# Two heads per step, softmax division after the product, and transfers in the order of the source: sparse attention feeding an expert layer

## The chip, the cores and the metric

The kernel runs on one core of one Trainium2 chip. The metric is the device time of one execution in microseconds (us), as the median of several runs. The engines are TensorE (PE in the profile; PEld is its loading of stationary operands), VectorE (DVE), ScalarE (ACT), GpSimd (POOL) and SyncE (SP), which here only issues transfers. SP's queue is written SPq.

## The reference

There are 8 batches of 8 heads, 576 queries and keys per head, 64 columns per head. Attention keeps only the scores that lie within tau (0.02) of the row's largest, and its output goes into an expert layer of 512 x 2048 x 512.

```python
scores = scale * np.matmul(q, k.transpose(0, 1, 3, 2))
thresh = np.max(scores, axis=-1, keepdims=True) - tau
scores = np.where(scores >= thresh, scores, -1000000000.0)
scores = scores - np.max(scores, axis=-1, keepdims=True)
attn = np.exp(scores)
attn = attn / (np.sum(attn, axis=-1, keepdims=True) + 1e-09)
attn_out = np.matmul(attn, v)
...
x = attn_out.transpose(0, 2, 1, 3).reshape(B * S, H * D)
h = x @ w_in
g = h * (1.0 / (1.0 + np.exp(-h)))
return g @ w_out
```

Because a score decides by a threshold whether a key counts at all, the kernel computes with values split into a high and a low part, which together carry more digits than one 16-bit or one fp32r value.

## The kernel before

**Visits and tiles.** Attention is worked off in visits. A visit is one pair of heads of one batch, and it is cut into tiles of 128 queries: four full ones for each head and a ninth that holds the last 64 queries of both heads. Batches 1 to 7 have four such visits each ("all"). Batch 0 has its visits in two halves, "low" (the first 256 queries) and "high" (the rest), so that the experts can start early; between them lie 12 free slots in which weights are decoded and split.

**Scores.** For one head, the high and the low part of q are stacked in the 128 partitions (64 rows each, `qstack`, made by `split_q`, lines 294 to 313), and k's high and low part (`split_k`, 315 to 321) each lie twice. So a tile needs two stationary loads of 128 rows per half of the keys: four matmuls of 128x128x288, or eight in the shared tile (`scores`, 385 to 409). For the stacking each of q and k is loaded twice from HBM (`load_qk`, 280 to 287).

**Softmax.** A tile takes these steps: DVE finds the row maximum (416) and the threshold (419); ACT takes the exponent (426); DVE masks and sums in one instruction (435) and inverts the sum (439, 443); ACT multiplies the row with it (448); POOL (ACT in the first 36 tiles) rounds to 16 bits (459) and subtracts for the low part (462, 465). SP then issues a transposing transfer (475) into `wT`. The scores tile `s` has two buffers of two PSUM banks; `w` has four buffers, `hl` three.

**Product with v and experts.** `av` (480 to 495) multiplies the transposed weights with v's two parts, both heads side by side in the array's columns, 128x64 each, in two ranges of 288 queries. `av_post` splits the result into x's two parts. The experts come as units: `h_unit` (12 matmuls, then tanh and two more steps), and quarters of `o_unit` (12 matmuls each). The units of a batch run while attention of the next batch goes on.

**Order.** The program is written as a loop over slots, one tile each (695 to 738). In each slot, softmax steps, planned loads and splits (`todo`), a number of expert units (`credit`) and products with v (`avs`) are emitted. The order on every engine is then set by a scheduler that simulates the program, with higher priority for scores and softmax. That includes the order of transfers in SP's queue. An engine, SP too, carries out its instructions strictly in that order, and one that waits holds those behind it.

The first visits ("low") work with plain fp32 scores and transposes on TensorE (`load_direct`, `scale_direct`, `soft3_direct`, `av_direct`).

Of the kernel before, what the change touches and what calls it, by code (L numbers as in the profile page):

```python
# [19 lines left out]
P = 128  # L20
# [6 lines left out]
WID = 320  # L27
EXPMASK = 0x7F800000
GB = 17  # buffers of g: a group of 16 and one ahead
WSPARE = 2  # raw weights lie this far ahead of the split ones, which take their place  # L30
LOAD = 5  # tiles that the loads of q and k run ahead
AV_LAG = 3  # tiles from a visit's last to its product with v
EARLY = 36  # tiles in which ACT still rounds the weights of attention for GpSimd
GAP, GAP1 = 12, 1  # free slots before batch 0's second visits and before batch 1
V_SLOT = 26  # batch 0's values are split from here on
# [6 lines left out]
# a visit of two heads: its tiles of 128 queries (4: the last 64 of both heads) for the  # L42
# first and the second head, and the query ranges that it completes
VISITS = {
    "low": ([0, 1], [0, 1], [(0, 256)]),
    "high": ([2, 3, 4], [2, 3], [(256, 320)]),
    "all": ([0, 1, 2, 3, 4], [0, 1, 2, 3], [(0, 288), (288, 288)]),
}
# [3 lines left out]
def attention_moe(  # L52
# [14 lines left out]
    xp = [ctx.enter_context(tc.tile_pool(name="x0", bufs=1))]  # L67
    stage_ctx = ExitStack()
    stage = stage_ctx.enter_context(tc.tile_pool(name="stage", bufs=2))
    ps_s = ctx.enter_context(tc.tile_pool(name="ps_s", bufs=2, space=PSUM))  # L70
# [3 lines left out]
    # three banks in turn; the last one is for the sums of the weights while they come in  # L74
# [20 lines left out]
    # stacks of (hi; lo) rows of q, with 64 zero columns for the shared tile  # L95
    qstack = []
    zeros = const.tile([P, 64], F32, name="zeros")
    nc.vector.memset(zeros, 0.0)
    for i in range(2):
        t = const.tile([P, S + 64], F32R, name=f"qstack{i}")  # L100
        zc = S if i % 2 == 0 else 0
        nc.vector.tensor_copy(t[:, zc : zc + 64], zeros)
        qstack.append(t)
# [32 lines left out]
    # ---------------------------------------------------------------- weights  # L136
# [47 lines left out]
        # sums of the magnitudes over the rows of four chunks, four columns at a time: they  # L184
        # bound h (w_in), w_out
# [33 lines left out]
    # ---------------------------------------------------------------- values  # L219
# [5 lines left out]
    def load_v(b, p):  # L225
        t = sb.tile([P, 2, 5, D], F32, tag="vraw", name=f"vraw_{b}_{p}", bufs=5)
        nc.sync.dma_start(out=t, in_=vL[b, :, 2 * p : 2 * p + 2])
        vraw[b, p] = t
# [37 lines left out]
    def split_v(b, p):  # L266
        t = vraw[b, p]
        s = vsc[b][:, 0:1]
        o = sb.tile([P, 2, 2, 5, D], F16, tag="v16", name=f"v16_{b}_{p}", bufs=4)
        nc.scalar.activation(o[:, 0], t, AF.Copy, scale=s)  # L270
        nc.vector.scalar_tensor_tensor(
            out=o[:, 1], in0=t, scalar=s, in1=o[:, 0], op0=ALU.mult, op1=ALU.subtract
        )
        v16[b, p] = o

    # ---------------------------------------------------------------- q and k
    qkraw = {}
    khl = {}

    def load_qk(v, h):  # L280
        b, hh = divmod(h, H)
        qr = sb.tile([P, S], F32, tag="qraw", name=f"qraw_{v}_{h}", bufs=2)
        kr = sb.tile([P, S], F32, tag="kraw", name=f"kraw_{v}_{h}", bufs=2)
        for r in range(2):
            nc.sync.dma_start(out=kr[r * D : (r + 1) * D, :], in_=kT[b, hh])
            nc.sync.dma_start(out=qr[r * D : (r + 1) * D, :], in_=qT[b, hh])
        qkraw[h] = qr, kr

    def qcol(h, i):
        """Column of query tile i in the stack (even: 0..3, last, zeros; odd: zeros, last,  # L290
        2, 3, 0, 1)."""
        return i * P if h % 2 == 0 else (0, 384, 512, 128, 256)[(i + 1) % 5]

    def split_q(h, tiles):
        qr = qkraw[h][0]
        odd = h % 2
        c0, c1 = 0, S
        if len(tiles) < 4:
            c0, c1 = (0, 320) if odd else (256, S)
# [45 lines left out]
    def soft3_direct(t):  # L345
# [4 lines left out]
        for k in range(4):  # L350
            nc.tensor.transpose(main[:, k, :], w[:, k * P : (k + 1) * P], ident)
# [429 lines left out]
```

## Time and profile before

| | |
|---|---|
| median of 3 runs | 1354.81 us (1354.6 to 1356.63) |
| span of the profiled execution | 1360.4 us |
| TensorE busy | 1183.7 us, 87% of the span |
| VectorE busy | 1002.8 us, 74% |
| ScalarE busy | 817.5 us, 60% |
| GpSimd busy | 789.9 us, 58% |
| DMA engines, mean busy share of the one large queue | 55.5% |
| mean granted TensorE clock | 0.950 of full speed |

The profile is of one execution. Busy times are unions of instruction times; matmuls are pipelined, and a busy PE is not one at its peak. A group row gives the source line, the engine, the operation, what is written and read, the shapes and the count; after the bar the busy time in us, the mean duration of one in ns, and the idle time of the engine just before them with what ended it.

### The profile page before, as it was taken

The numbers are of one execution on the slowest core, as the hardware profiler recorded it, in microseconds if no ns is written. First come the engines' busy times: TensorE is split into PE (matmuls) and PEld (weight loads), VectorE is DVE, ScalarE is ACT, GpSimd is POOL, SyncE is SP. The second block draws the span as 40 slices with busy tenths as digits, with TensorE's granted clock in tenths as the row PEclk, the third lists the DMA queues.
The fourth block names the chain that finished last, engine by engine and source line by source line (L and its number), as shares of the span: only waits on it lengthen the run. The fifth ranks groups of instructions, "written<-read, shape, count | busy, mean of one in ns | idle before, by whom it ended". The sixth has DMA issues, their size and how long they took to land.

```text
span 1360.4 us, 26858 instructions
## 1 busy us (share of the span) xinstructions
PE 1183.7 (87%) x9392; PEld 899.9 (66%) x9392; DVE 1002.8 (74%) x2619; ACT 817.5 (60%) x1493; POOL 789.9 (58%) x964
## 2 busy tenths in 40 slices
PE   3774787898599979898899969899799999999998
PEld 2453555666477757676677757677577777777777
DVE  4987997897598967968497856869478787872421
ACT  3776775675476756656375745757367666662432
POOL 2647984787478656754476646556467666661000
PEclk9887888999799999999899979999799999999999
DMA  6454955778467656664475556565466565543000
GB/s 226 140 185 125 197 129 94 146 139 170 88 133 155 122 106 129 131 128 86 99 132 124 118 96 136 101 127 121 82 122 116 115 129 115 106 88 53 6 19 18
DMA packets 363479, 158.15 MB, mean 116 GB/s; under 512 B 329552, under 2 KB 338256, under 8 KB 363344
## 3 DMA queue, kind: packets, MB, share of 16 engines
q1 hardware_dynamic: 363344, 156.43, 55.5%
q8 instruction: 74, 1.21, 0.4%
q14 instruction: 61, 0.50, 0.1%
HBM read 66.72 MB, written 9.44 MB: 56 GB/s over the span
## 4 chain that ended last, share of the span: by engine, by line
DVE 35%; PE 34%; issue 13%; ACT 6%; POOL 6%; DMA 5%; SPq 2%; POOLq 0%; ACTq 0%; DVEq 0%
PE o L562 15%; PE h L524 8%; DVE w L435 8%; DVE sm L416 6%; DVE gbuf L547 6%; PE s L406 5%; PE a L490 5%; DVE qstack L310 3%; DVE th L533 3%; DMA vraw<-in_vL 2%; DMA wT<-hl 2%; ACT w L426 2%; POOL hl L459 2%; POOL hl L462 2%; ACT w L448 2%
## 5 line engine op out<-in xcount | busy, mean ns | idle before, releaser
L524 PE MATMUL h<-x,wst 128*128 128x288 f16 (+2 forms) x3072 | 422.3, 290 | 22.6 <-DVE th L533 19.1
L562 PE MATMUL o<-gbuf,wst 128*128 128x288 f16 (+2 forms) x3072 | 419.4, 293 | 22.4 <-DVE gbuf L547 16.1
L562 PEld LDWEIGHTS <-wst 128*128 128x128 f16 x3072 | 296.4, 100 | 117.1 <-issue 27.1
L459 POOL TENSOR_SCALAR hl<-w 128x576 f16<-128x576 f32 x264 | 187.3, 710 | 317.9 <-ACT w L448 69.1
L524 PEld LDWEIGHTS <-wst 128*128 128x128 f16 x3072 | 290.7, 99 | 119.2 <-issue 37.5
L462 POOL TENSOR_TENSOR hl<-w,hl 128x512 f16<-128x512 f32 x272 | 332.0, 1220 | 28.0 <-issue 13.9
L426 ACT ACTIVATE w<-s,sm 128x576 f32<-128x576 f32 x288 | 211.0, 736 | 204.5 <-POOL hl L465 135.4
L435 DVE SCALAR_TENSOR_TENSOR w<-s,sm,w 128x576 f32<-128x576 f32 x288 | 232.6, 810 | 110.4 <-ACT w L426 108.7
L448 ACT ACTIVATE w<-w,sm 128x576 f32<-128x576 f32 x288 | 218.2, 770 | 86.5 <-DVE sm L443 81.6
L416 DVE TENSOR_REDUCE sm<-s 128x1 f32<-128x576 f32 x288 | 215.1, 748 | 44.4 <-PE s L406 42.3
L406 PE MATMUL s<-khi,qstack 128*128 128x288 f32 x608 | 160.4, 346 | 70.0 <-DVE w L435 36.9
L547 DVE SCALAR_TENSOR_TENSOR gbuf<-th,gbuf 128x288 f16<-128x288 f32 (+2 forms) x256 | 167.3, 656 | 20.9 <-ACT gbuf L541 20.2
L406 PEld LDWEIGHTS s<-khi,qstack 128*128 128x128 f32 x608 | 98.5, 198 | 98.8 <-issue 71.4
L490 PE MATMUL a<-wT,v 128*64 128x288 f16 (+1 forms) x1680 | 142.4, 294 | 16.1 <-DMA wT<-hl 15.0
L532 ACT ACTIVATE th<-h,msc 128x288 f32<-128x288 f32 (+2 forms) x256 | 126.3, 495 | 49.5 <-DVE gbuf L547 30.0
L541 ACT ACTIVATE gbuf<-th 128x288 f16<-128x288 f32 (+2 forms) x252 | 109.9, 438 | 44.5 <-DVE th L533 43.9
L406 PE MATMUL s<-klo,qstack 128*128 128x288 f32 x608 | 134.2, 304 | 0.0
L533 DVE SCALAR_TENSOR_TENSOR th<-th,h 128x288 f32<-128x288 f32 (+2 forms) x256 | 113.2, 444 | 27.6 <-ACT th L532 25.4
L490 PEld LDWEIGHTS <-v 128*64 128x64 f16 x1680 | 91.3, 110 | 56.7 <-issue 41.9
L465 POOL TENSOR_TENSOR hl<-w,hl 128x64 f16<-128x64 f32 x272 | 115.3, 424 | 0.0
L406 PEld LDWEIGHTS s<-klo,qstack 128*128 128x128 f32 x608 | 102.2, 197 | 0.0
L320 POOL TENSOR_TENSOR klo<-kraw,khi 128x576 fp32r<-128x576 f32 x64 | 95.6, 1493 | 1.4 <-ACT khi L318 1.3
(82 smaller groups left out, 868.8 us busy)
## 6 DMA issues: line engine op xcount, KB each, us to landing
qraw<-in_qT SPq DMA_DIRECT2D x128, 144.0 KB, 3.0
kraw<-in_kT SPq DMA_DIRECT2D x128, 144.0 KB, 3.0
vraw<-in_vL SPq DMA_DIRECT2D x32, 320.0 KB, 3.5
wraw<-in_w_out SPq DMA_DIRECT2D x16, 512.0 KB, 4.0
out_t<-ot SPq DMA_DIRECT2D x56, 144.0 KB, 2.0
wT<-hl SPq DMA_TRANSPOSE x304, 3.3
gbuf<-in_w_in SPq DMA_DIRECT2D x8, 512.0 KB, 5.1
wraw<-in_w_in SPq DMA_DIRECT2D x8, 512.0 KB, 4.9
```

The source lines that it names most:

```text
L406: nc.tensor.matmul(s_ps[:, j, :HALF], lhs, kk[:, j * HALF : (j + 1) * HALF], start=(n == 0), stop=(n == len(seq) - 1),)
L416: nc.vector.tensor_reduce(out=negm, in_=s_ps[:, :, :HALF], op=ALU.max, axis=AX.XY, negate=True)
L426: nc.scalar.activation(wtile[t].rearrange("p (j c) -> p j c", j=2), sps[t][:, :, :HALF], AF.Exp, bias=small[t][:, 0:1],)
L435: nc.vector.scalar_tensor_tensor(out=w3, in0=s_ps[:, :, :HALF], scalar=sm[:, 1:2], in1=w3, op0=ALU.is_ge, op1=ALU.mult, accum_out=sm[:, 2:3],)
L448: nc.scalar.activation(w, w, AF.Copy, scale=r)
L459: nc.gpsimd.tensor_scalar(out=fl[:, 0:S], in0=w, scalar1=1.0, scalar2=1.0, op0=ALU.mult, op1=ALU.mult)
L462: nc.gpsimd.tensor_tensor(out=fl[:, 640:1152], in0=w[:, 0:512], in1=fl[:, 0:512], op=ALU.subtract)
L490: nc.tensor.matmul(a_ps[odd * D : (odd + 1) * D, :n], vt[:, lo_v, odd, kv, :], wT[v, b * H + 2 * p + odd][:, kw, c0 - base : c0 - base + n ...
L524: nc.tensor.matmul(ph[:, :n], wi(c, f, lo_w), x16[b, lo_x][:, c, c0 : c0 + n], start=(k == 0), stop=(k == 11),)
L533: nc.vector.scalar_tensor_tensor(out=th[:, :n], in0=th[:, :n], scalar=1.0, in1=ph[:, :n], op0=ALU.add, op1=ALU.mult,)
L547: nc.vector.scalar_tensor_tensor(out=g[:, 1, :n], in0=th[:, :n], scalar=2.0**-14, in1=g[:, 0, :n], op0=ALU.mult, op1=ALU.subtract,)
L562: nc.tensor.matmul(ps[:, :n], wo(f, d, lo_w), g[:, lo_g, :n], start=(f == 0 and k == 0), stop=(f == NF - 1 and k == 2),)
```

## The change

1. **Both heads of a pair in one step.** A step is one tile of 128 queries of both heads (or the shared tile of the last 64 queries, as before). The pair's q and k lie one head in partitions 0 to 63, the other in 64 to 127, so they are loaded once and split once per visit. The four products of high and low parts become four matmuls of 64 rows per head and half of the keys, and the heads alternate. The maximum, the rounding and the subtraction cover both heads (1152 columns) in one instruction; exponent and masked sum stay one per head. A step takes two slots, the shared one takes one slot.
2. **Buffers.** `s` has one buffer of four banks; `w` two and `hl` two buffers of both heads; raw q and k have one each. In the loop, the scores of the next step are now emitted behind the masked sums of the step.
3. **Division per visit.** Weights are no longer divided row by row. The sums of a range of queries are collected, inverted at once (`invert_sums`), written to DRAM in pieces of 4 bytes, read back three slots later, spread over 64 partitions per head (`load_rows`), and multiplied with the result of the product with v on DVE; ACT rounds it and POOL subtracts. The "low" visits still divide by row.
4. **Engines.** The threshold moves from DVE to POOL, rounding of the weights from POOL to ACT, x's low part from DVE to POOL.
5. **Values.** The 1152 transposed rows of a head (576 high, 576 low) now lie without a gap, so that v's high part is needed a second time, moved by 64 rows; two transfers inside SBUF make it. v is loaded once for its maximum and once more for its splitting.
6. **Ranges** are 256 and 320 queries for all visits; the product follows five slots behind.
7. **Transfers.** SP's queue is in the order of the source (`manual_schedule`); the other engines are still ordered by the scheduler.

The core of the diff:

```diff
+    ctx.enter_context(tc.manual_schedule(engines={mybir.EngineType.SP}))
...
-    ps_s = ctx.enter_context(tc.tile_pool(name="ps_s", bufs=2, space=PSUM))
+    ps_s = ctx.enter_context(tc.tile_pool(name="ps_s", bufs=1, space=PSUM))
...
     def scores(t):
-        v, parts = tiles[t]
-        s_ps = ps_s.tile([P, 2, 512], F32, tag="s", name=f"s_{t}")
+        v, i = steps[t]
+        s_ps = ps_s.tile([P, 2, 2, 512], F32, tag="s", name=f"s_{t}")
...
+            qh, ql, kh, kl = qk16[v]
+            seq = [(qh, kh), (qh, kl), (ql, kh), (ql, kl)]
+        w = P if i == 4 else D
+        for n, (qq, kk) in enumerate(seq):
             for j in range(2):
...
+                for h in range(heads(t)):
+                    r = slice(h * w, (h + 1) * w)
+                    nc.tensor.matmul(
+                        s_ps[:, h, j, :HALF], qq[r, i * P : (i + 1) * P],
+                        kk[r, j * HALF : (j + 1) * HALF],
+                        start=(n == 0), stop=(n == len(seq) - 1),
+                    )
...
+            out=sm[:, 0:nh], in_=s_ps[:, :nh, :, :HALF], op=ALU.max, axis=AX.XY, negate=True
+        )
+        nc.gpsimd.tensor_scalar(
+            out=sm[:, 2 : 2 + nh], in0=sm[:, 0:nh], scalar1=-1.0, scalar2=ntau,
+            op0=ALU.mult, op1=ALU.add,
+        )
...
+        nc.scalar.activation(hl[:, :nh, 0:S], w[:, :nh], AF.Copy)
         nc.gpsimd.tensor_tensor(
...
+            out=hl[:, :nh, S : 2 * S], in0=w[:, :nh], in1=hl[:, :nh, 0:S], op=ALU.subtract
+        )
```

The new functions for the sums:

```python
def invert_sums(v, a, b):
    if v not in rdram:
        r = sb.tile([P, 9], F32, tag="rsum", name=f"rsum_{v}", bufs=2)
        rdram[v] = r, dram.tile([2, S], F32, tag="rs", name=f"rs_{v}", bufs=4)
    r, d = rdram[v]
    nc.vector.tensor_scalar(
        out=r[:, a:b], in0=sums[v][:, a:b], scalar1=1e-9, scalar2=None, op0=ALU.add
    )
    nc.vector.reciprocal(out=r[:, a:b], in_=r[:, a:b])
    for h in range(2):
        if a < 8:
            nc.sync.dma_start(
                out=d[h, 64 * a : 64 * min(b, 8)].rearrange("(i p) -> p i", p=P),
                in_=r[:, a + h : min(b, 8) : 2],
            )
        if b == 9:
            nc.sync.dma_start(
                out=d[h, S - D :].rearrange("(p o) -> p o", o=1),
                in_=r[h * D : (h + 1) * D, 8:9],
            )

def load_rows(v, g):
    c0, n = RANGES[g]
    _, d = rdram[v]
    R = sb.tile([P, WID], F32, tag="rows", name=f"rows_{v}_{g}", bufs=2)
    for h in range(2):
        nc.sync.dma_start(
            out=R[h * D : (h + 1) * D, :n], in_=d[h, c0 : c0 + n].partition_broadcast(D)
        )
    rows[v, g] = R
```

The splitting of v and of x:

```diff
-        nc.scalar.activation(o[:, 0], t, AF.Copy, scale=s)
+        nc.scalar.activation(hi[:, :, 0:5, :], t, AF.Copy, scale=s)
...
+            out=lo, in0=t, scalar=s, in1=hi[:, :, 0:5, :], op0=ALU.mult, op1=ALU.subtract
+        )
+        nc.sync.dma_start(out=hi[0:D, :, 5:9, :], in_=hi[D:P, :, 0:4, :])
+        nc.sync.dma_start(out=hi[D:P, :, 5:9, :], in_=hi[0:D, :, 1:5, :])
...
+        x = sb.tile([P, WID], F32, tag="th", name=f"x32_{v}_{c0}", bufs=4)
+        nc.vector.tensor_tensor(
+            out=x[:, :n], in0=a_ps[:, :n], in1=rows.pop((v, g))[:, :n], op=ALU.mult
+        )
+        nc.scalar.activation(hi, x[:, :n], AF.Copy)
+        nc.gpsimd.tensor_tensor(out=lo, in0=x[:, :n], in1=hi, op=ALU.subtract)
```

More of the change, by code (lines that the diff above doesn't have):

```diff
@@ L273, in split_v @@
         )
-        v16[b, p] = o
+        nc.sync.dma_start(out=hi[0:D, :, 5:9, :], in_=hi[D:P, :, 0:4, :])
+        nc.sync.dma_start(out=hi[D:P, :, 5:9, :], in_=hi[0:D, :, 1:5, :])
+        v16[b, p] = hi, lo
     qkraw = {}
[L278 to L287, printed above, removed]
@@ L433, in soft2 @@
         sm, w = small[t], wtile[t]
[L434 to L438 removed]
+        if v in direct:
+            total = sm[:, 4:6]
+        else:
+            if v not in sums:
+                sums[v] = sb.tile([P, 9], F32, tag="sums", name=f"sums_{v}", bufs=3)
+            total = sums[v][:, 2 * i : 2 * i + nh]
@@ new lines, in soft2 @@
+        for h in range(nh):
+            w3 = w[:, h].rearrange("p (j c) -> p j c", j=2)
+            nc.vector.scalar_tensor_tensor(
+                out=w3, in0=s_ps[:, h, :, :HALF], scalar=sm[:, 2 + h : 3 + h], in1=w3,
+                op0=ALU.is_ge, op1=ALU.mult, accum_out=total[:, h : h + 1],
+            )
+        if v not in direct:
+            small.pop(t)
+            return
+        nc.vector.tensor_scalar(
+            out=sm[:, 6:8], in0=total, scalar1=1e-9, scalar2=2.0**-12, op0=ALU.add, op1=ALU.mult
+        )
@@ L690, in live @@
     def live(t):
-        return 0 <= t < NT and tiles[t] is not None
+        return 0 <= t < len(steps) and steps[t] is not None
     scores(0)
-    t = 0
-    while t < NT + 8 or units or ready:
+    k = 0
+    while k < len(steps) or units or ready or avs:
+        t = begin[k] if k < len(steps) else NT + k - len(steps)
+        nxt = begin[k + 1] if k + 1 < len(steps) else max(t + 1, NT)
         while ready and ready[0][0] <= t:
```

406 lines of the change are left out of this document (185 added, 221 removed).

## The prediction

> **What bounds the kernel now.** I read the profile page first, then stretches of the span, then the groups of instructions, and last the timelines of TensorE and of SP's queue.
>
> ```profile
> span 1360.4 us, 26858 instructions
> PE 1183.7 (87%) x9392; PEld 899.9 (66%) x9392; DVE 1002.8 (74%) x2619; ACT 817.5 (60%) x1493; POOL 789.9 (58%) x964
> ```
>
> Stretches; columns: length, busy time of PE, PEld, DVE, ACT, POOL, then granted clock, DMA share, GB/s:
>
> ```profile
> 0.00:200.00 200.00, 127.41 (x761) 87.33 (x761) 168.44 (x397) 131.74 (x242) 130.91 (x138) 0.85 0.62 167
> 200.00:1000.00 800.00, 702.87 (x5658) 537.07 (x5658) 611.83 (x1645) 490.22 (x877) 501.23 (x631) 0.95 0.61 120
> 1000.00:1240.00 240.00, 236.75 (x2003) 182.80 (x2001) 192.69 (x513) 158.99 (x298) 157.72 (x197) 1.00 0.58 110
> 1240.00:1360.00 120.00, 116.62 (x976) 92.66 (x973) 29.86 (x66) 36.59 (x78) 0.00 (x0) 1.00 0.06 18
> ```
>
> Three parts. Up to 200 us DVE leads (168 of 200). From 200 to 1000 us PE is busy 703 of 800: 97 us idle, and the clock of 0.95 costs another 0.05 x 703 = 35 us. After 1000 us PE is full, the last 120 us with experts alone. Only 73 + 132 us can be had; the rest is matmuls that the change keeps. Who makes PE idle? PE's own waits name DVE:
>
> ```profile
> PE s L406 <- DVE w L435: 36.9, 26, 10.6
> PE h L524 <- DVE th L533: 19.1, 20, 2.8
> PE o L562 <- DVE gbuf L547: 16.1, 6, 5.0
> ACT w L426 <- POOL hl L465: 135.4, 54, 14.4
> ```
>
> The last row is the way round through POOL: ACT's exponent waits for a w buffer that POOL's slow splitting still holds. A batch has one reduction over partitions on POOL. Between two of them that lie two batches apart:
>
> ```profile
> 643.85 0.38 POOL L113 PARTITION_ALL_REDUCE v_all<-v_one  x1 [5.84 <-issue]
> ...
> 957.33 0.38 POOL L113 PARTITION_ALL_REDUCE v_all<-v_one  x1 [5.91 <-issue]
> ```
>
> That is 313.5 us, so 157 us a batch, 39 us a visit (a quarter: one pair of heads) and 4.4 us a slot of the plan (36 to a batch).
>
> **The vector engines, per visit.** Group rows: busy us, mean ns, idle before.
>
> ```profile
> L459 POOL TENSOR_SCALAR hl<-w 128x576 f16<-128x576 f32 x264 | 187.3, 710 | 317.9 <-ACT w L448 69.1
> L462 POOL TENSOR_TENSOR hl<-w,hl 128x512 f16<-128x512 f32 x272 | 332.0, 1220 | 28.0 <-issue 13.9
> L426 ACT ACTIVATE w<-s,sm 128x576 f32<-128x576 f32 x288 | 211.0, 736 | 204.5 <-POOL hl L465 135.4
> L435 DVE SCALAR_TENSOR_TENSOR w<-s,sm,w 128x576 f32<-128x576 f32 x288 | 232.6, 810 | 110.4 <-ACT w L426 108.7
> L448 ACT ACTIVATE w<-w,sm 128x576 f32<-128x576 f32 x288 | 218.2, 770 | 86.5 <-DVE sm L443 81.6
> L416 DVE TENSOR_REDUCE sm<-s 128x1 f32<-128x576 f32 x288 | 215.1, 748 | 44.4 <-PE s L406 42.3
> L465 POOL TENSOR_TENSOR hl<-w,hl 128x64 f16<-128x64 f32 x272 | 115.3, 424 | 0.0
> L320 POOL TENSOR_TENSOR klo<-kraw,khi 128x576 fp32r<-128x576 f32 x64 | 95.6, 1493 | 1.4 <-ACT khi L318 1.3
> L310 DVE SCALAR_TENSOR_TENSOR qstack<-qraw,gate,qstack 64x576 fp32r<-64x576 f32 x56 | 68.8, 1228 | 5.8 <-ACT qstack L309 3.9 <-DMA wT<-hl 0.3
> L419 DVE TENSOR_SCALAR sm<-sm,ntau 128x1 f32<-128x1 f32 x288 | 59.0, 207 | 2.8
> L443 DVE RECIPROCAL sm<-sm 128x1 f32<-128x1 f32 x288 | 44.2, 156 | 2.5
> L439 DVE TENSOR_SCALAR sm<-sm 128x1 f32<-128x1 f32 x288 | 41.4, 145 | 1.2
> L271 DVE SCALAR_TENSOR_TENSOR v<-vraw,v_sc,v 128x640 f16<-128x640 f32 x32 | 33.3, 1041 | 2.4 <-ACT v L270 2.3
> L435 DVE DVE_READ_ACCUMULATOR w<-s,sm,w 128x1 f32 x288 | 23.3, 81 | 0.0
> L457 ACT ACTIVATE hl<-w 128x576 f16<-128x576 f32 x8 | 5.4, 674 | 0.0
> ```
>
> *DVE.* Before, nine tiles of 748 + 207 + 810 + 81 + 145 + 156 = 2147 ns and two q splits of 1228: 21.8 us. After, four maxima over 1152 columns and one over 576. No row has 1152; it lies between 748 and 2 x 748, and I take 1.34 us, a little below two. Thresholds leave (to POOL); the nine masked sums of 891 ns stay; sums are inverted twice a visit, not nine times (2 x 301 ns); one q split of 128x640 takes 1.1 us (between L271 and L310). That is 6.1 + 8.0 + 0.6 + 1.1 = 15.8. The two products after AV cost as the two subtractions before. **Saved: 6 us a visit, 168 us in 28.** In batch 0 I count 10 us.
>
> *ACT.* The nine divisions (6.9 us) go; rounding comes from POOL as four of 1152 columns (1.14 each, below two of 674) and one of 674: 5.2. One k and one q copy fewer (1.4). Saved: about 3 us.
>
> *POOL.* Before 9 x (710 + 1220 + 424) + 2 x 1493 = 24.2 us. After, L462 and L465 give 1.78 ns a column, so 1152 columns take 2.36 us and 576 take 1.33: 10.8; one klo 1.5; five thresholds at L465's 0.42, the smallest POOL row of this form, 2.1; two x splits 1.6. Sum 16.0, saved 8.
>
> **TensorE.** Expert and AV matmuls keep their columns. The shared step of the last 64 queries stays at 8. A two-head step has 16 score matmuls of 64 rows in place of 8 of 128, the heads alternating between array halves.
>
> ```profile
> 1098.42 0.79 PE L524 MATMUL h<-x,wst 128*128 128x288 f16 x5
> 1102.14 0.43 PE L406 MATMUL s<-khi,qstack 128*128 128x288 f32 x2
> 1102.67 1.16 PE L562 MATMUL o<-gbuf,wst 128*128 128x288 f16 x8
> 317.64 1.29 PE L490 MATMUL a<-wT,v 128*64 128x288 f16 x17
> 1098.18 0.11 PEld L490 LDWEIGHTS <-v 128*64 128x64 f16 x1 [0.24 <-issue]
> ```
>
> Four score matmuls take 1102.67 - 1102.14 = 0.53 us, 0.13 each. The 17 AV matmuls of 288 columns last 1.29 us; less the 0.3 that a matmul lasts by itself (0.43 - 0.13 in the s row) that is 1.0/16 = 0.06 each, half a score matmul: two column halves of the array do run together. No row has two row halves; bounds are 0 us extra (together) and 8 x 0.13 = 1.04 us a step (in turn). I take 0, nearest to the AV row, which is also two half-arrays at work.
>
> There is a price at the border. One AV matmul alone holds PE from 1098.18 to 1098.42, with 0.24 us of idle loading ahead of it. I take 0.3 us for going into halves and back (0 if the border is free): 28 x 4 + 4 x 2 = 120 two-head steps give **+36 us**. The Trainium skill, TensorEngine Tiling, Key Properties, says that a change of tiling mode drains TensorE. The AV rows agree for column halves; no run here shows row halves. By that rule the 36 us stand, without it the sum falls by 36.
>
> **The new wait.** s now has one buffer of four banks, where it had two of two. So the next step's scores wait until both masked sums are done, and DVE's maximum waits for those scores.
>
> ```profile
> 1002.58 0.74 DVE L416 TENSOR_REDUCE sm<-s 128x1 f32<-128x576 f32 x1
> 1003.41 0.74 ACT L426 ACTIVATE w<-s,sm 128x576 f32<-128x576 f32 x1 [0.17 <-DVE sm L416]
> ```
>
> A hop between engines is about 0.1 us. One round: scores 1.04 and the last one's 0.3, maximum 1.34, first exponent 0.74 (the threshold of 0.42 beside it, the second exponent behind), two masked sums 1.78, four hops: 5.6 us; the one-head step 4.1. A visit is 4 x 5.6 + 4.1 = 26.5 us, under the 39 us of now. I cost it at nothing: experts fill PE and DVE meanwhile. Without that cover the four chains gain the next rival.
>
> **SP's queue.** Columns: start, length, issues.
>
> ```profile
> 1016.22 1.10 SPq L286 DMA_DIRECT2D qraw<-in_qT  x2
> 1022.20 14.88 SPq L475 DMA_TRANSPOSE wT<-hl  x7
> 1044.42 1.22 SPq L475 DMA_TRANSPOSE wT<-hl  x1
> ```
>
> Transposes stay at ten a visit, 1.22 to 2.13 us each. Other issues, at 0.55: before 8 of q and k, 1 of v, 2 outputs; after 2, 2 of v, 2 copies of split v, 6 writes of sums, 4 reads of rows, 2 outputs. So 21.3 + 11 x 0.55 = 27 us becomes 21.3 + 18 x 0.55 = 31, still below a visit. Each keeps its place in the source: a transpose waits behind an output of the experts, and split v's copies wait on ACT. The writes move 4 bytes a piece; bounds 0.55 and 2.13 us, I take 0.55, the plain issue. The sums are read back three slots (13 us) after the write, and a plain transfer lands in about 3 us:
>
> ```profile
> qraw<-in_qT SPq DMA_DIRECT2D x128, 144.0 KB, 3.0
> vraw<-in_vL SPq DMA_DIRECT2D x32, 320.0 KB, 3.5
> ```
>
> Bytes: before 8 x 144 + 320 = 1472 KB a visit, after 288 + 320 + 2 x 320 = 1248 KB and the small copies. With the DMA engines at 0.61, I cost that at nothing. Raw q and k now have one buffer each: their load is issued six slots ahead of a visit, just when the visit before has split its own (two or three slots ahead of its start, nine slots back). If that split is late, SP stands, and with it every transpose behind; this belongs to the SP rival below.
>
> **Small edits together.** x gets one more step (product on DVE, copy on ACT, subtraction on POOL, with 0.8 us more on POOL): it delays the experts of a new batch by about a microsecond per range, hidden while those of the batch before are left. Two w and two hl buffers of two heads hold as much as four and nearly as much as three of one; POOL's shorter work pays for the lost turn. AV waits five slots, not three, which the same experts cover. In the first part, thresholds and inversions of 16 + 20 tiles shrink to 8 + 12 steps, and batch 0's values are split later: that is the 10 us, with bounds 0 and 20.
>
> **Sum.** Of the 132 us in the middle I take half, 66: DVE's load between 200 and 1240 us falls by a fifth (168 of 612 + 193), and the three waits for DVE quoted first add up to 72. First part -10, border +36: 1360.4 - 66 - 10 + 36 = 1320. The profiled span lies 6 us above the median of 1354.81, so 1315; with the last batch's first 256 queries ready some steps earlier, I say **1310**, with 1270 to 1345 for this case.
>
> **Rivals.** (1) *Row halves in turn:* 120 x 1.04 = 125 us more, of which remaining idle takes about 30: 1405. For it: each of the 16 still has a load of 128 columns of its own, and no row shows row halves at once. Against: the AV pairs. The Trainium skill, TensorE: Matmul & The Clock Gate, Part 3, says that a load overlaps running matmuls when the row group differs; no run here shows it, and it speaks for 1310. (2) *The single s buffer becomes the bound, ending slower:* it decides once a two-head step passes (38.1 - 4.1)/4 = 8.5 us, where 38.1 is the visit I forecast: 39.2 - (66 - 36)/28. The clean round has 5.6; four handovers, each behind another operation of 0.4 to 0.8 us on DVE or ACT (the sizes of L465 and L435) or a 2.36 us subtraction on POOL ahead of the threshold, could bring 0.9 each, 9.2 in all, so a visit of 40.9 and 28 x 2.8 = 78 us: 1390. PE would wait on L435's successor and the clock dip. (3) *SP's queue:* six writes at 2.13 make it 31 + 9.5 = 40.7 a visit, 28 x 2.6 = 73 us: 1385. (4) *PE gets dense:* three quarters of the 132 and half the border price: 1360 - 99 - 15 + 18 - 6 = 1258. (5) *Savings stay off the path* and border costs equal them: no change.
>
> **Chances.** Forecast 0.44, (4) 0.13, (1) 0.17, (2) 0.15, (3) 0.07, (5) 0.04. The range 1255 to 1410 leaves out half of (4) and (1) and a little beyond. A measurement of this kernel tells 0.2% from no change: faster 0.58, same 0.05, slower 0.37.
>
> **What would show it.** Right: DVE near 830 us busy, POOL near 560, PE idle from 200 to 1000 us near 50, and 16 score matmuls in 1.1 to 1.4 us. Wrong: those 16 in over 2 us (1); PE or DVE idle at s with batches over 158 us (2); SP issuing without a gap, transposes late (3). A lower clock in the middle than 0.95 would undo the sum too.

## The result, and the profile after

The changed kernel takes **1783.1 us** (median of 4 runs, 1778.28 to 1786.58). The kernel before takes 1355.72 (4 runs, 1354.6 to 1362.9). The ratio is **1.312, 95% interval 1.3076 to 1.3165**: slower by 427 us. The forecast was 1310, faster, with 1255 to 1410 as its range.

The page of the changed kernel: span, busy times, and groups (busy us, mean ns | idle of the engine just before, with what ended it).

```profile
span 1782.6 us, 27206 instructions
...
PE 1294.0 (73%) x10352; PEld 957.6 (54%) x10352; DVE 926.0 (52%) x1736; ACT 745.8 (42%) x1289; POOL 545.3 (31%) x486
...
L398 ACT ACTIVATE w<-s,sm 128x576 f32<-128x576 f32 x288 | 199.2, 737 | 339.3 <-DVE sm L386 325.2
L416 DVE SCALAR_TENSOR_TENSOR w<-s,sm,w 128x576 f32<-128x576 f32 x288 | 225.0, 814 | 222.3 <-ACT w L398 162.7
L386 DVE TENSOR_REDUCE sm<-s 128x2 f32<-128x1152 f32 (+1 forms) x160 | 196.9, 1231 | 152.0 <-PE s L374 152.0
...
L575 DVE SCALAR_TENSOR_TENSOR gbuf<-th,gbuf 128x256 f16<-128x256 f32 (+1 forms) x256 | 209.5, 832 | 63.6 <-ACT gbuf L569 61.5
L374 PE MATMUL s<-khi,qhi 64*128 64x288 f32 (+1 forms) x544 | 92.5, 385 | 188.6 <-DVE w L416 188.2
...
L230 DVE TENSOR_REDUCE vmx<-vraw 128x1 f32<-128x640 f32 x32 | 26.1, 816 | 127.4 <-DMA vraw<-in_vL 127.3
L536 DVE TENSOR_TENSOR x<-a,rows 128x320 f32<-128x320 f32 (+1 forms) x60 | 27.3, 455 | 123.9 <-DMA rows<-rs 113.3
```

All three vector engines do less than before (DVE 926 for 1003, ACT 746 for 818, POOL 545 for 790), and no engine is full. Such a page tells of a kernel bound by waits, and the idle column says by which. Lines 398, 416, 386 and 374 form a ring: exponent waits for the maximum, masked sum for the exponent, the next scores for the masked sum, the next maximum for the scores. In each row the idle time is of the order of the busy time. Two more rows have grown or are new: DVE stands 127 us for a DMA ahead of v's maximum (18 us before the change) and 113 us ahead of the first product with the sums.

A long stretch in the middle; columns: length, busy PE, PEld, DVE, ACT, POOL, then granted clock, DMA share, GB/s:

```profile
400.00:1500.00 1100.00, 822.06 (x6764) 615.11 (x6763) 566.12 (x1054) 452.13 (x777) 332.03 (x282) 0.87 0.60 91
```

PE is idle 278 of 1100 us, about twice the idle share of before (97 of 800), and the granted clock is 0.87 there, 0.95 before. The loss is spread over the whole steady part. The reductions over partitions mark the batches:

```profile
1006.02 0.38 POOL L104 PARTITION_ALL_REDUCE v_all<-v_one  x1 [7.62 <-issue]
1213.41 0.38 POOL L104 PARTITION_ALL_REDUCE v_all<-v_one  x1 [6.61 <-issue]
```

That is 207.4 us a batch, 51.8 a visit, where before had 39.2 and the forecast 38.1. Over 28 visits 28 x 12.6 = 353 of the 427 us, if this batch stands for the others; the rest would lie ahead of and behind this part.

**One round of the new ring**, in the timeline (start, length, engine, line, operation, count, idle before it; some rows are left out):

```profile
901.06 1.37 ACT L398 ACTIVATE w<-s,sm 128x576 f32<-128x576 f32 x2 [1.46 <-DVE sm L386]
902.55 0.82 DVE L416 SCALAR_TENSOR_TENSOR w<-s,sm,w 128x576 f32<-128x576 f32 x1 [1.25 <-ACT w L398]
904.62 0.53 PE L374 MATMUL s<-khi,qhi 64*128 64x288 f32 x4
905.52 0.42 PE L374 MATMUL s<-klo,qlo 64*128 64x288 f32 x4
905.45 2.38 POOL L479 TENSOR_TENSOR hl<-w,hl 128x1152 f16<-128x1152 f32 x1 [4.11 <-ACT hl L478]
905.65 2.46 DVE L575 SCALAR_TENSOR_TENSOR gbuf<-th,gbuf 128x256 f16<-128x256 f32 x1 [0.25 <-ACT gbuf L569]
907.79 1.58 POOL L295 TENSOR_TENSOR klo<-kraw,khi 128x576 fp32r<-128x576 f32 x1
908.03 0.41 DVE L561 SCALAR_TENSOR_TENSOR th<-th,h 128x256 f32<-128x256 f32 x1
908.36 1.29 DVE L575 SCALAR_TENSOR_TENSOR gbuf<-th,gbuf 128x256 f16<-128x256 f32 x1
909.58 0.87 DVE L304 SCALAR_TENSOR_TENSOR qlo<-qraw,gate,qhi 128x640 fp32r<-128x640 f32 x1
910.37 1.34 DVE L386 TENSOR_REDUCE sm<-s 128x2 f32<-128x1152 f32 x1
918.76 1.34 DVE L386 TENSOR_REDUCE sm<-s 128x2 f32<-128x1152 f32 x1
```

The maximum ahead of these rows starts at 899.62, the next one at 910.37: 10.75 us for a round that the prediction put at 5.6. The round behind it takes 8.39, to 918.76. Two things lengthen it. The first masked sum starts only behind *both* exponents (901.06 + 1.37 = 902.43, start 902.55); the prediction had the second one beside it. And the scores are there at 905.94, but DVE has meanwhile taken up the experts' products and a q split, and comes to the maximum 4.4 us later. Two of these products, which take 0.41 by themselves, last 2.46 and 1.29 us here; each ends 0.28 us behind a subtraction on POOL (905.45 + 2.38 = 907.83, 907.79 + 1.58 = 909.37).

**What stands on DVE for SP.** Four of the waits of SP's queue (us in total, times, longest):

```profile
SPq L601 <- ACT ot L599: 226.4, 29, 32.3
SPq L494 <- POOL sm L389: 178.7, 29, 21.4
SPq L494 <- POOL hl L479: 178.2, 46, 13.7
SPq L458 <- DMA rs<-rsum: 66.0, 37, 7.6
```

SP isn't full: these four waits alone hold it for 649 of 1783 us. It stands, in the order of the source, at an output of the experts, at a transpose whose weights aren't ready, or at the reading back of sums, with the loads that DVE needs behind it. That SP stands is not new: in the kernel before, its three longest waits, for transposes and outputs, make 509 of 1360 us. What lies behind a wait has to be looked at. An instance of a late load, in SP's timeline and in DVE's:

```profile
885.08 0.59 SPq L443 DMA_DIRECT2D rs<-rsum  x1
885.72 0.48 SPq L448 DMA_DIRECT2D rs<-rsum  x1
886.24 0.58 SPq L224 DMA_DIRECT2D vraw<-in_vL  x1
891.47 5.53 SPq L494 DMA_TRANSPOSE wT<-hl  x2
```

```profile
897.31 0.82 DVE L230 TENSOR_REDUCE vmx<-vraw 128x1 f32<-128x640 f32 x1 [8.59 <-DMA vraw<-in_vL]
899.62 1.35 DVE L386 TENSOR_REDUCE sm<-s 128x2 f32<-128x1152 f32 x1
```

The last load of v issued ahead of this maximum goes out at 886.24, 11 us before it. DVE stands 8.59 us at a maximum that no score needs for some time, and the softmax maximum, behind it in DVE's order, stands as well. So a late load comes into the ring.

But this load wasn't late in SP's queue. It was issued right behind the sums' writes of 4 bytes a piece, and its last DMA packet ended only at 896.5. In the trace's DMA packets this is the rule: of the 60 loads of v, the 12 that go out within 0.05 us behind such a write need 9.3 to 10.1 us from the end of the issue to their last packet, the other 48 need 2.1 to 5.1. Single packets of 2560 bytes take up to 8.6 us, for a median of 0.1. At these 12 loads DVE stands 100 of the 127 us ahead of v's maximum. Why packets behind such writes are slow, no run here shows.

### The profile page after: what moved, and what is told of

It reads as the page before. It is cut to its first block, busy times and chain, and to the rows that moved or that the text cites. A ratio compares the mean times of both kernels' runs of the same rounds, so it can differ in the third digit from the quotient of the medians.

```text
span 1782.6 us, 27206 instructions
## 1 busy us (share of the span) xinstructions
PE 1294.0 (73%) x10352; PEld 957.6 (54%) x10352; DVE 926.0 (52%) x1736; ACT 745.8 (42%) x1289; POOL 545.3 (31%) x486
## 3 DMA queue, kind: packets, MB, share of 16 engines
q8 instruction: 82, 1.34, 0.4%
## 5 line engine op out<-in xcount | busy, mean ns | idle before, releaser
L552 PE MATMUL h<-x,wst 128*128 128x320 f16 (+1 forms) x3072 | 457.0, 307 | 126.1 <-DVE th L561 85.9
L479 POOL TENSOR_TENSOR hl<-w,hl 128x1152 f16<-128x1152 f32 (+1 forms) x152 | 326.9, 2151 | 549.1 <-ACT hl L478 438.5
L590 PE MATMUL o<-gbuf,wst 128*128 128x320 f16 (+1 forms) x3072 | 409.7, 293 | 26.3 <-DVE gbuf L575 15.2
L386 DVE TENSOR_REDUCE sm<-s 128x2 f32<-128x1152 f32 (+1 forms) x160 | 196.9, 1231 | 152.0 <-PE s L374 152.0
L478 ACT ACTIVATE hl<-w 128x1152 f16<-128x1152 f32 (+1 forms) x152 | 161.5, 1062 | 225.4 <-DVE w L416 171.2
L575 DVE SCALAR_TENSOR_TENSOR gbuf<-th,gbuf 128x256 f16<-128x256 f32 (+1 forms) x256 | 209.5, 832 | 63.6 <-ACT gbuf L569 61.5
L509 PE MATMUL a<-wT,vhi 128*64 128x320 f16 (+1 forms) x1080 | 116.0, 330 | 89.1 <-DMA wT<-hl 82.4
L389 POOL TENSOR_SCALAR sm<-sm,ntau 128x2 f32<-128x2 f32 (+1 forms) x160 | 51.8, 324 | 365.0 <-DVE sm L386 310.3
L569 ACT ACTIVATE gbuf<-th 128x320 f16<-128x320 f32 (+1 forms) x252 | 106.4, 437 | 105.8 <-DVE th L561 104.8
L560 ACT ACTIVATE th<-h,msc 128x256 f32<-128x256 f32 (+1 forms) x256 | 121.5, 495 | 47.7 <-PE h L552 24.4
L561 DVE SCALAR_TENSOR_TENSOR th<-th,h 128x256 f32<-128x256 f32 (+1 forms) x256 | 111.2, 447 | 35.9 <-ACT th L560 34.1
L230 DVE TENSOR_REDUCE vmx<-vraw 128x1 f32<-128x640 f32 x32 | 26.1, 816 | 127.4 <-DMA vraw<-in_vL 127.3
```

The costliest lines, as they stand in the source:

```text
L386: nc.vector.tensor_reduce(out=sm[:, 0:nh], in_=s_ps[:, :nh, :, :HALF], op=ALU.max, axis=AX.XY, negate=True)
L478: nc.scalar.activation(hl[:, :nh, 0:S], w[:, :nh], AF.Copy)
L479: nc.gpsimd.tensor_tensor(out=hl[:, :nh, S : 2 * S], in0=w[:, :nh], in1=hl[:, :nh, 0:S], op=ALU.subtract)
L509: nc.tensor.matmul(a_ps[odd * D : (odd + 1) * D, :n], vt[:, odd, kw, :], wT[v, odd, g][:, kw, :], start=(k == 0), stop=(k == len(seq) - 1),)
L552: nc.tensor.matmul(ph[:, :n], wi(c, f, lo_w), x16[b, lo_x][:, c, c0 : c0 + n], start=(k == 0), stop=(k == 11),)
L560: nc.scalar.activation(th[:, :n], ph[:, :n], AF.Tanh, scale=moe_sc[b][:, 0:1])
```

## Experiments

Two theories. **S**: the one buffer of s closes a ring that nothing covers. **Q**: the source order of SP's queue, with the new small transfers in it, makes loads late, and DVE stands for them. Differences are to the kernel that each edits, 1783.1 for the changed one and the run of before beside each experiment (1356 to 1363). Except for the last they are single runs without an interval; runs of one kernel lie up to 9 us (before), 8 us (after) or 13 us (the last experiment) apart.

**The two in the kernel before, and one undone in the changed one.**

e1 takes the source order out of the changed kernel, e2 puts it into the kernel before, and e3 gives the kernel before one s buffer (of one head, as its tiles are).

```diff
-    ctx.enter_context(tc.manual_schedule(engines={mybir.EngineType.SP}))
```

```diff
+    ctx.enter_context(tc.manual_schedule(engines={mybir.EngineType.SP}))
```

```diff
-    ps_s = ctx.enter_context(tc.tile_pool(name="ps_s", bufs=2, space=PSUM))
+    ps_s = ctx.enter_context(tc.tile_pool(name="ps_s", bufs=1, space=PSUM))
```

> The changed kernel, with the scheduler ordering SP's queue again; all else of the change stays. Theory Q (the queue): in the order of the source the transfers come late, and the engines that work strictly in order stand for them (DVE 127 us for v's load and 113 us for the rows of sums, PE 82 us for transposed weights); then this run falls to 1330 to 1480 us, with both DVE waits under 60 us together. Theory S (the single s buffer): the round scores, maximum, exponent, masked sums is what lasts 10.6 us a step; then this run stays at 1680 to 1790 us.

> The kernel before, with only its SP queue put into the order of the source. Theory Q: the transfers come late here too, 1500 us or more. Theory S: SP's order is no cause, within 3% of 1355 us.

> The kernel before, with one buffer of s (a tile of one head, two banks) in place of two. Its round is scores 0.53 + 0.3, maximum 0.75, exponent 0.74, masked sum 0.89, some hops: about 3.6 us against 4.4 us per tile now. Theory S: as in the changed kernel the round grows with what stands between, 1550 us or more. Theory Q: under 1420 us.

Measured: e1 **1851.54** (68 slower), e2 **1426.61** (+64), e3 **1700.86** (+338). In the kernel before, one s buffer is by itself worth most of the loss, and its waits have the pattern of the changed kernel (waits of e3, in us, times, longest):

```profile
DVE sm L416 <- PE s L406: 293.0, 177, 8.4
...
PE s L406 <- DVE w L435: 227.0, 81, 6.1
```

The source order costs too, but less. In e1, handing SP back to the scheduler made it worse; DVE's wait for v's loads fell from 127 to 71 us, and others grew (waits of e1):

```profile
PE a L508 <- DMA wT<-hl: 264.5, 51, 12.7
SPq L457 <- DMA rs<-rsum: 382.9, 95, 9.6
```

In the scheduler's order SP stands 383 us for the reading back of sums (66 in the changed kernel), with the transposes behind it. So Q as I had put it, that the order alone is at fault, is refuted for the changed kernel.

**Opening the ring in the changed kernel.** e4 compares the exponents instead of the scores in the masked sum, so that s is free after the exponent (it keeps other keys than attention does). e5 gives each head its own two-bank s, two buffers, with the maximum per head.

```diff
-                out=w3, in0=s_ps[:, h, :, :HALF], scalar=sm[:, 2 + h : 3 + h], in1=w3,
+                out=w3, in0=w3, scalar=sm[:, 2 + h : 3 + h], in1=w3,
```

```diff
-    ps_s = ctx.enter_context(tc.tile_pool(name="ps_s", bufs=1, space=PSUM))
+    ps_s = ctx.enter_context(tc.tile_pool(name="ps_s", bufs=2, space=PSUM))
...
-        s_ps = ps_s.tile([P, 2, 2, 512], F32, tag="s", name=f"s_{t}")
...
+        for h in range(heads(t)):
+            s_ps = ps_s.tile([P, 2, 512], F32, tag="s", name=f"s_{t}_{h}")
```

> The changed kernel, with the masked sum reading w in place of s (so the comparison is made on the exponents, not on the scores): s is free for the next scores once the two exponents are done, and 1.8 us of masked sums leave the round. Theory S: a step gets 1.8 us or more shorter, 28 x 4.5 x 1.8 = 225 us, so 1560 us or less. Theory Q: transfers as late as before, 1700 us or more.

> The changed kernel, with the single s buffer undone: the same four banks as two buffers of one head each, scores, maxima and thresholds head by head, so that one head's scores can be made while the other head is in softmax. Its price: row halves no longer work side by side (about 1 us more of TensorE in each of 120 two-head steps) and 0.15 us more of DVE. Theory S (the single s buffer): the 42 us a batch or so that one buffer cost in the kernel before come back, less the price: 1480 to 1600 us. Theory Q (late transfers at which DVE stands) and theory B (DVE stands while POOL's 2.4 us subtraction runs): 1720 us or more.

Measured: e4 **1714.63** (−68), e5 **1754.2** (−29). Undoing S alone gives back little; S alone is refuted as well. Part of the time went into the other wait: DVE stands 170 us ahead of v's maximum in e4 and 203 in e5, for 127 in the changed kernel. This speaks for two causes, one behind the other, each hiding what the other costs; e12 and e13 test it.

**One suspected cost at a time.** e6: an ACT copy in place of POOL's subtraction, so that the low part of the weights is left out. e7: constant sums in place of reading back, so that the division is left out but the writes stay, and v's maximum four slots later in the source. e8: the outputs issued by ACT, not by SP. e9: e5 and e8.

```diff
-        nc.gpsimd.tensor_tensor(
-            out=hl[:, :nh, S : 2 * S], in0=w[:, :nh], in1=hl[:, :nh, 0:S], op=ALU.subtract
-        )
+        nc.scalar.activation(hl[:, :nh, S : 2 * S], w[:, :nh], AF.Copy)
```

```diff
+        rows[v, g] = rconst
...
-                at(u + 6 * p - 30, lambda b=b, p=p: vmax(b, p))
+                at(u + 6 * p - 26, lambda b=b, p=p: vmax(b, p))
```

```diff
-            nc.sync.dma_start(out=outT[d * P : (d + 1) * P, c : c + n], in_=o[:, :n])
+            nc.scalar.dma_start(out=outT[d * P : (d + 1) * P, c : c + n], in_=o[:, :n])
```

> The changed kernel; ACT writes a copy of w where POOL subtracted, so the low part of the weights is left out and POOL's 327 us of subtractions go. Theory B: DVE's operations on g (832 ns each, 656 before the change) fall under 500 ns, the round loses about 1 us a step, 1600 to 1700 us. Theories S and Q: g's operations may get short, but the time stays within 50 us of 1783.

> The changed kernel, with DVE's two waits for transfers taken out: v's maximum is taken four slots later, and the rows of inverted sums are a constant (the reading back and so the division are left out; the writing stays). Theory Q: DVE's 240 us of standing go and the time falls with them, 1520 to 1620 us. Theory S: the round sets the pace and the waits lay beside it, 1720 us or more. Part of each: in between, in proportion.

> The changed kernel; the 64 transfers of the experts' output are issued by ACT behind the operation that makes the output, so SP, otherwise in the order of the source, no longer waits for the experts (226 us in 29 waits). Theory Q (transfers held back in SP's queue): transposes and loads come earlier, 1700 us or less. Theory S (the single s buffer): within 50 us of 1783.

> The same output transfers on ACT, in the kernel with s as two buffers of one head each (1754 us). Theory SQ (either of the two, one s buffer or SP's order, is enough to hold a batch at 205 us, and only both undone set it free): 1650 us or less. If the pace has another cause: 1720 us or more.

Measured: e6 **1747.38** (−36), e7 **1760.48** (−23), e8 **1734.3** (−49), e9 **1672.72** (−82 to e5, −110 in all). e7 was a miss as an experiment: it was to end the wait for v's first load, and the wait stayed (137.6 us, 127.3 in the changed kernel), so that what it says of reading back alone is little. It does bear on why the loads are slow: it keeps the writes, and 100 of the 137.6 us are again at loads issued right behind them. So slow loads don't need the reading back. e6 takes POOL's subtraction out as the main cause. e9 points to S and Q working together: outputs off SP are worth 49 with the ring closed and 82 with it open.

**Both in the kernel before (e10), and the scheduler's order with the ring open (e11).** e10 is e2 and e3 together; e11 is e5 without the line of `manual_schedule`.

> The kernel before, with one buffer of s and with SP in the order of the source, its two losses of 338 and 64 us taken together. If the changed kernel's loss is these two and its savings on DVE, ACT and POOL lie off the path, this comes near it: 1720 to 1820 us. If the two together cost no more than the larger one alone: about 1700 us. If they strengthen each other: over 1850 us.

> The changed kernel with two s buffers of one head each and with SP's queue left to the scheduler: both suspects undone, the rest of the change stays (both heads split at once, division per visit, one buffer of raw q and k, work moved between engines). Theory SQ: 1350 to 1520 us. If something else in the change sets the pace: 1700 us or more.

Measured: e10 **1741.06**, +380, with none of the rest of the change in it. e11 **1794.18**, 40 slower than e5: the scheduler's order isn't the cure here. As in e1, the reading back of sums holds SP's queue in e11, 210 us in 58 times.

**Taking the late transfers out.** e12 drops from the changed kernel the whole way of the sums through DRAM and v's first load with its maximum in batches 1 to 7, and issues outputs from ACT. e13 is e12 with e5's two buffers; e14 is e13 with e6's copy. e15 drops the sums' way alone, e16 the first load of v alone. Their edits are those above and these:

```diff
-        for h in range(2):
-            if a < 8:
-                nc.sync.dma_start(
...
+        rows[v, g] = rconst
...
+        for later in range(1, B):
+            vsc[later] = vsc[0]
...
-                at(u + 6 * p - 36, lambda b=b, p=p: load_v(b, p))
-                at(u + 6 * p - 30, lambda b=b, p=p: vmax(b, p))
```

> The changed kernel without the transfers at which DVE and SP stand: no sums through DRAM (rows are a constant, so no division), no second load and no maximum of v in batches 1 to 7 (batch 0's scale is used), outputs issued by ACT. One s buffer stays. Theory S (one s buffer alone holds the pace): 1650 us or more. Theory Q (the late transfers hold it): 1500 us or less. If either holds it alone: 1650 or more here, and far less in the next run.

> The same, and s as two buffers of one head each (row halves in turn). Theory SQ (each of the two holds the pace when the other is gone): 1350 to 1500 us. If POOL's two-head subtraction, during which DVE stands, or the buffers of w and hl hold it: 1600 us or more.

> The same as the run before, and ACT's copy in place of POOL's subtraction of the weights (the low part is left out). Theory B (DVE stands while POOL runs, 120 times up to 2.4 us): at least 80 us below the run before. Otherwise within 30 us of it.

> The changed kernel without the way of the sums through DRAM alone (no writes, no reads, rows are a constant, so no division); v's first load, its maximum and the outputs stay as they are. Of the 228 us that the three took together, theory W (SP stands up to 8 us at the read for the 4-byte writes, and DVE for the rows): more than half, 1650 us or less. Theory V (DVE stands for v's first load): 1720 us or more.

> The changed kernel without v's first load and maximum in batches 1 to 7 alone (batch 0's scale is used). Theory V: more than half of the 228 us, 1650 us or less. Theory W: 1720 us or more.

Measured: e12 **1554.9** (−228), e13 **1434.82** (−120 more), e14 **1402.31** (−33 more); e15 **1640.28** (−143), e16 **1670.2** (−113). In e15, without the sums' writes and reads, no load of v needs more than 5.3 us to its last packet, and DVE's wait ahead of v's maximum falls from 127 to:

```profile
DVE vmx L230 <- DMA vraw<-in_vL: 51.5, 23, 4.2
```

So the sums' way (W) is behind most of what V names as well, and what e16 gains comes in part from no longer standing at loads that the writes made slow; its waits for the sums stay. The same stretch of 800 us in e12, e13 and e14, columns as above:

```profile
400.00:1200.00 800.00, 678.02 (x5892) 517.82 (x5890) 507.91 (x879) 392.36 (x687) 280.30 (x235) 0.93 0.46 92
```

```profile
400.00:1200.00 800.00, 779.92 (x6319) 602.15 (x6318) 537.35 (x1027) 432.66 (x727) 337.41 (x340) 0.99 0.50 101
```

```profile
400.00:1200.00 800.00, 797.26 (x6518) 616.62 (x6516) 465.53 (x1046) 530.33 (x847) 116.63 (x243) 1.00 0.52 102
```

PE goes from 678 to 780 to 797 of 800 and the clock from 0.93 to 1.00: with late loads, ring and POOL's hold on DVE gone, PE hardly idles. The three are worth 228 + 120 + 33 = 381 us from the side of the changed kernel. That e10 gave 380 from the side of the kernel before is chance: it has the ring and the source order, but no sums through DRAM. The parts overlap (143, 113 and 49 by themselves, 228 together), so no split among them is exact. Also, e12 to e14 leave out v's maximum in seven batches, which the kernel before has (26 us on DVE in all eight). They keep what else the change brought: the single buffers of raw q and k, two of w and hl, the threshold on POOL, the longer lag of the product. With PE busy 797 of 800 us, these hardly cost anything there.

e1, e2, e9, e12, e14 and e16 met neither of the ranges set beforehand, and e11 refuted SQ as it was put, since the scheduler's order brought a wait of its own.

What is left in e14, 46 us above before, looks like TensorE's own time, and part of it belongs to the experiment. With each head's scores in a tile of its own, the row halves no longer run together:

```profile
802.56 0.53 PE L377 MATMUL s<-khi,qhi 64*128 64x288 f32 x2
...
803.46 0.42 PE L377 MATMUL s<-klo,qlo 64*128 64x288 f32 x2
```

Eight take 802.56 to 803.88 here, as long as sixteen in the changed kernel (904.62 to 905.94). A second group of up to 1.3 us in 120 steps would be up to 156 us. That is an estimate from these rows; PE's busy time in e14 is 1325.5 for 1183.7 before, 142 more.

**A version that beats both.** e8's edit, made in the kernel before:

> The kernel before, with the experts' outputs issued by ACT. In the changed kernel this gave 49 us. Where SP's queue is already in the scheduler's order, its 160 us of waiting for outputs lie mostly in the tail, where nothing is behind them: within 0.5% of the kernel before; if SP's waits held transposes back here too, 1% or more faster.

Measured: e17 **1354.11** (10 runs) beside 1361.85 of before (13 runs), ratio **0.9948, 95% interval 0.9923 to 0.9974**: half a per cent faster than the kernel before, and so faster than both. That is between the two ranges set beforehand. The wait that it takes off SP's queue was in the kernel before:

```profile
SPq L573 <- ACT ot L571: 160.0, 27, 30.9
```

Here lies a lesson on Q: 160 us of SP standing at outputs cost the kernel before some 8 us, 226 us of it cost the changed one 49. Of the 160, 113 lie behind 1240 us, where the experts run alone; of the 226, 124 lie ahead of 1500 us, with attention behind them. A wait in a queue has no price of its own; it has that of the entry behind it and of whoever needs that entry.

## Why the prediction was wrong

| step of the prediction | forecast | measured |
|---|---|---|
| maximum over 1152 columns | 1.34 us | 1.351 |
| POOL's subtraction over 1152 | 2.36 us | 2.376 |
| q split of 128x640 | 1.1 us | 1.045 |
| POOL busy | about 560 us | 545.3 |
| DVE busy | about 830 us | 926.0 |
| 16 score matmuls of 64 rows | 1.1 to 1.4 us | 1.32 |
| a round of two heads | 5.6 us, hidden | 10.75 and 8.39 in the rows above |
| SP's issues, a visit | 31 us | 26 us (batch from 1006 to 1213 us) |
| landing of a plain load | about 3 us | 2.1 to 5.1 us, 9.3 to 10.1 behind the sums' writes |
| middle part | −66 us | PE idles more, 278 of 1100 us |

The rows of the first three, by form, and DVE's product as it was before:

```profile
L386 DVE TENSOR_REDUCE sm<-s 128x2 f32<-128x1152 f32 x128 | 172.9, 1351 | 135.4 <-PE s L374 135.4
L479 POOL TENSOR_TENSOR hl<-w,hl 128x1152 f16<-128x1152 f32 x120 | 285.2, 2376 | 452.6 <-ACT hl L478 348.8 <-issue 101.0 <-DMA wT<-hl 2.8
L304 DVE SCALAR_TENSOR_TENSOR qlo<-qraw,gate,qhi 128x640 fp32r<-128x640 f32 x28 | 29.3, 1045 | 35.0 <-ACT qhi L302 35.0
```

```profile
L547 DVE SCALAR_TENSOR_TENSOR gbuf<-th,gbuf 128x288 f16<-128x288 f32 (+2 forms) x256 | 167.3, 656 | 20.9 <-ACT gbuf L541 20.2
```

**What held.** The three durations taken from rows of other widths were within about 5%. The row halves do run together (rival 1 is out). The price of the border stays open: in the changed kernel TensorE's loading stands 0.25 us on going into halves and 0.16 on coming back, which is near the 0.3, but its matmuls show no gap there (those of the AV product ahead run to 904.68), so the rows don't show that the 36 us were paid. The Trainium skill, TensorE: Matmul & The Clock Gate, Part 3, says that a load overlaps running matmuls where the row groups differ; 16 matmuls of half height in the time of 8 agree.

```profile
904.61 0.30 PEld L374 LDWEIGHTS s<-khi,qhi 64*128 64x128 f32 x4 [0.25 <-PE a L509]
905.87 2.52 PEld L552 LDWEIGHTS <-wst 128*128 128x128 f16 x24 [0.16 <-issue]
```

**Where it failed, first: "The new wait ... I cost it at nothing: experts fill PE and DVE meanwhile."** That sentence has the answer in it. The experts do fill DVE, and that's the harm: their operations stand in DVE's order between the end of the scores and the maximum, and with one buffer no second tile is under way meanwhile. Rival (2) named the mechanism and a threshold of 8.5 us a step, then priced a handover at 0.9 us and the step at 9.2. With the shared step at 934.10 − 928.14 = 5.96 us, where its maximum starts at 928.14 and the next at 934.10, the mean two-head step is about (51.8 − 5.96)/4 = 11.5 us. The clean round was a bound from below, and I compared that with the time at hand. One s buffer costs 338 us in the kernel before (e3), and undoing it is worth 120 in the changed one once the late transfers are gone (e13).

```profile
928.14 0.76 DVE L386 TENSOR_REDUCE sm<-s 128x1 f32<-128x576 f32 x1 [4.90 <-PE s L374]
934.10 1.36 DVE L386 TENSOR_REDUCE sm<-s 128x2 f32<-128x1152 f32 x1 [3.01 <-PE s L374]
```

**Second: SP's queue, "31, still below a visit".** I priced a queue by the time that its issues take. Its price was in its waits and in how late its loads land. The issues took even less than 31 us; but "a transpose waits behind an output of the experts" stood in that paragraph without a number, and in the changed kernel outputs alone hold SP for 226 us. The writes of 4 bytes got "0.55, the plain issue", and nothing for the load behind them, though "a plain transfer lands in about 3 us" was the figure that all loads had to keep. Rival (3) looked for six dear writes and an SP that issues without a gap. The writes were cheap to issue (0.5 us each); what they cost was the 10 us of the load behind them and the reading back. The sums' way is worth 143 us by itself (e15); with v's first load and the outputs it is 228 (e12), which includes the work on v that e12 leaves out.

**Third, a size: DVE's saving.** 926 for 830. The experts' product went from 656 to 832 ns a piece: 256 x 176 = 45 of the 96 us. Most of the rest is in the counting: the forecast took durations off a busy time that counts overlapping instructions once. Added up singly, DVE's instructions fall from 1159 to 1018 us, 141 less; their overlap falls too, from 156 to 92 us.

**Fourth: rivals taken one at a time.** (2) and (3) got 0.15 and 0.07 as separate cases at 1390 and 1385. They came together, and as the rows read they fed each other: a load that is late holds DVE, DVE is in the ring, and the ring makes POOL and ACT late, for which SP stands. That opening the ring is worth 29 us with the late transfers (e5) and 120 without them (e13) agrees. The range had no place for both. The direction, slower, had a chance of 0.37, but from rivals that ended at 1385 to 1405.

**Still open.** Why a load right behind the 4-byte writes needs 10 us: the writes, their place in DRAM and the reading back were taken out together in e15, the reading back alone in e7. And the last 46 us of e14 weren't split by a run. That the scheduler's order of SP's queue is worse than the source's in the changed kernel, when in the kernel before it is better by 64, is read from waits alone: SP stands 383 us (e1) and 210 us (e11) at the reading back of sums, which the kernel before doesn't have.

## What to carry to other kernels

When a buffer between engines goes from two to one, write out the round it closes, with what stands ahead of each of its instructions in each engine's order, and hold *that* against the time at hand; the clean round is only the lower bound. Price a queue that works in order by what its entries wait for, and look at who waits for the entry behind. Ask of a late load first whether it was issued late or landed late: here most of DVE's wait was at loads that had been issued early enough for a landing in 3 us or nearly so, but right behind transfers of very small pieces. If undoing one suspect gives little, undo two at once before you drop either.

## What the runs showed of the hardware that was not expected

**POOL holds DVE for a whole instruction.** The product of two tiles in SBUF on DVE takes 0.41 us by itself (at 911.64), and 2.46 when POOL's subtraction has started 0.20 us ahead of it (905.65 to 908.11, POOL's from 905.45 to 907.83). With POOL's subtraction gone, its mean falls from 833 ns (e13) to 480:

```profile
L564 DVE SCALAR_TENSOR_TENSOR gbuf<-th,gbuf 128x256 f16<-128x256 f32 (+1 forms) x256 | 120.5, 480 | 76.6 <-ACT gbuf L558 75.1
```

One subtraction over both heads, 2.38 us in place of 1.22 and 0.42 for each, saves POOL 0.9 us a step, and the longest hold that this subtraction can put on DVE doubled. In time it counts for little here: without it, DVE is busy 114 us less (940 in e13, 826 in e14), and the kernel is 33 us faster (single runs). The Trainium skill, SBUF — State Buffer, Who interferes with whom, says that a VectorE instruction with two SBUF inputs and a GpSimd one that reads SBUF exclude each other for a whole instruction, and that the order of issue decides who stands. These rows agree.

**Writes of 4-byte pieces make the transfer behind them late, and reading them back stands the queue.** Writes that carry 1 KB or less, issued in 0.5 us, made a load of 320 KB right behind them land 9.3 to 10.1 us after its issue in 12 cases of 12, for 2.1 to 5.1 elsewhere. The reads of the inverted sums held SP 37 times, 66 us in all and up to 7.6 each; in the scheduler's order (e1) 95 times, 383 us in all and up to 9.6 each. The prediction counted on three slots, 13 us, between write and read, and on landings of about 3 us.
